# Transform pieces at other steps: where a schedule written out by hand puts the FFT pieces between the matmuls of the next layer

## The chip, the cores and the metric

One core of one Trainium2 chip. The metric is device time in microseconds of one execution; the median of three runs is compared.

## The reference

A Fourier filter along the sequence, and then a feed-forward layer with a leaky activation. Eight batches, 3008 positions, 256 channels, 2048 hidden units.

```python
batch, seq, dim = (8, 3008, 256)
X = np.fft.rfft(x, axis=1)
Y = X * (filt_r + 1j * filt_i)[None, :, :]
y = np.fft.irfft(Y, n=x.shape[1], axis=1)          # float32
h = y.reshape(24064, 256) @ moe_w_in               # 256 -> 2048
g = np.maximum(h, 0.0) + moe_alpha * np.minimum(h, 0.0)
out = (g @ moe_w_out).astype(np.float32)           # 2048 -> 256
```

## The kernel before, in words

The layer runs on 48 blocks of 512 (or 384) positions. A block takes 16 **steps**, 768 steps in all; 96 steps go over one batch. In a step the kernel issues first what its plan has for that step, then `up(j)` of the current block (two matmuls into `hps`, L478; after every second step ScalarE takes them out into `gtb`, L486, and VectorE applies the activation, L489 and L490), then the matmuls of the block before, a sixteenth of them. Some blocks (FAST, every second one from block 12, and the last ones) multiply by `wout` with seven products in place of eight (`seven`, L537); they need sums of quarters of `gtb`, `sums(w, h)`: z1 and z2 by VectorE (L498, L500) into `ss`, and two additions by DMA from GpSimd (L502, L504). The tuple SUMS says at which step of its block (counted from the block's first) each is issued.

Between them stand the **pieces** of the Fourier transform of the coming batches, split as 47 x 64. For each batch:

- `load_x` (L148): four x loads from GpSimd, with a cast, into four buffers `xs`. For batch b+1 they are put at steps p+6, p+10, p+16 and p+20, where p = 96(b-1) for batch b.
- `piece_a`, 16 times (L190): one matmul on `xs`; ScalarE takes the result into one of two buffers `asb`. After every fourth, `save_a` (L195) writes a buffer to DRAM (`a_dram`) from SyncE.
- `turn_a` (L202): four reads of `a_dram` with rows and columns exchanged, 384 KB each in runs of 512 bytes, into `at`. SyncE issues them once the last write has landed and the last reader of `at` is done. This is the turned array.
- `piece_b`, 12 times, the forward pairs kp = 0 to 11 (L210): two matmuls on `at`; VectorE multiplies the result by the filter into `ww` and `uu` (L213, L214); then two DMAs from GpSimd add the halves of `ww` onto `uu` (L216).
- `piece_c`, 12 times, the inverse pairs (L228): two matmuls on `uu`; ScalarE takes the result into `v`. After every third, `turn_c` (L237) writes to `v_dram` in four DMAs from SyncE; after the last of them three `load_z` (L246) read it back into `zt`, on the same queue. A fourth `load_z` follows later.
- `piece_d`, 16 times (L253): four matmuls on `zt`; ScalarE takes the result into `yT`, which `up` reads. The batch of this plan is read from step p+96 on.

Pieces a, b, c and d share two PSUM banks; the string BANKS says for each piece, in the order of issue, which one it uses. STEPS_A, STEPS_B, STEPS_C and STEPS_D give the steps of the four kinds of pieces relative to p, for batches with index 3 to 7 (index 3 has its own list of a, and its b not before 2 kp - 12). Index 0, 1 and 2 have plans of their own (`plan_fft`). The steps of a for batch b+1 fall into the steps of batch b: step -84 of it is p+12.

All engines issue in the order of the program. SyncE carries the output stores (L447), L195, L202, L237 and L246; GpSimd carries L148, L216, L502 and L504. A tile with several buffers is reused in turn: the write of a new one waits for the readers of the old one. `uu` has four buffers, `ww` three, `at` and `v` one, `zt` three.

Of the kernel before, what the change touches and what calls it, by code (L numbers as in the profile page):

```python
# [20 lines left out]
NH = 32  # L21
BANKS = (
    "010101010101010101010101010101001011100011011010100100100101010101010101010101010101010101010101"
    "010101010101010101010010101010101000111101010010010010101011010101011101010101010101010100011001"
    "011010110011010101011001101011010101010101010100101010110010110010101010101001100101001010101010"
    "101010110101010011010011010101010101100110101101010101010101010010101011001011001010101010100110"
    "01010010101010101010101010110010101001100100101010101010"
)
STEPS_A = (-81, -80, -78, -72, -70, -67, -62, -61, -56, -52, -52, -50, -50, -45, -44, -42)
STEPS_B = (-20, -16, -9, 3, 7, 16, 29, 36, 40, 47, 57, 57)  # L30
STEPS_C = (-1, 5, 12, 14, 21, 33, 37, 48, 63, 63, 66, 66)
STEPS_D = (83, 85, 85, 86, 89, 93, 94, 99, 105, 107, 109, 118, 119, 129, 139, 146)
FAST = frozenset([n for n in range(12,42) if n%6 in (0,2,4)]+[42,43,44,45])
SUMS = ((11, 1, 0), (12, 3, 0), (17, 1, 1), (18, 3, 1), (19, 2, 0), (19, 2, 1), (20, 4, 0), (20, 4, 1))
TAIL = ((12, 1, 0), (12, 3, 0), (18, 1, 1), (18, 3, 1), (18, 2, 0), (18, 2, 1), (20, 4, 0), (21, 4, 1))
LAG = 16
AF = mybir.ActivationFunctionType
# [43 lines left out]
def kernel(  # L81
# [63 lines left out]
    def load_x(b, c):  # L145
        xs = p_x.tile([2 * N1, 8 * D], FP16, name="xs")
        for h in range(2):
            nc.gpsimd.dma_start(out=xs[h * N1 : h * N1 + N1], in_=xrow(b, h, c))  # L148
        return xs
# [445 lines left out]
    def put(step, fn, *args):  # L595
        plan.setdefault(step, []).append((fn, args))

    def plan_fft(b, a0, ga, ta, b0, gap, add, lag, d0, quarters, x_at):
        f = Fft(b)
        for i in range(16):  # L600
            put(int(a0 + ga * i), f.piece_a, i, on_act)
        for c in range(4):
            put(int(a0 + ga * (4 * c + 3)), f.save_a, c)
            if b + 1 < NB:
                put(x_at[c],
                    lambda b=b, c=c: xc.update({(b + 1, c): load_x(b + 1, c)}))
        for q in range(quarters):
            w = NK1 // quarters
            put(ta, f.turn_a, nc.sync, w * q, w * q + w)
        bs = [b0 + (2 * int(gap * kp / 2) if add else int(gap * kp)) for kp in range(12)]  # L610
        for kp in range(12):
            put(bs[kp], f.piece_b, kp)
            put(bs[kp] + lag, f.piece_c, kp, on_act)
        for q in range(4):
            put(bs[3 * q + 2] + lag + 1, f.turn_c, q)
        for i in range(16):
            put(d0 + min(i, 4) + 2 * max(i - 4, 0), f.piece_d, i, on_act)
        put(d0 + 5, f.load_z, 3)
# [9 lines left out]
    for i in range(4):  # L628
        put(26 + 3 * i, neg, 6 * i, 6 * i + 6)
    plan_fft(1, 16, 1, 32, 40, 3, 0, 6, 92, 4, (20, 24, 74, 75))  # L630
    plan_fft(2, 66, 2, 97, 109, 4.5, 8, 12, 187, 4, (110, 114, 118, 122))
    for b in range(3, NB):
        p = 96 * (b - 1)
        f = Fft(b)
        steps_a = STEPS_A if b > 3 else [int(2.4 * i) - 68 if i < 8 else 2 * i - 60 for i in range(16)]
        steps_b = STEPS_B if b > 3 else [max(st, 2 * kp - 12) for kp, st in enumerate(STEPS_B)]
        for i in range(16):
            put(p + steps_a[i], f.piece_a, i, on_act)
            if i % 4 == 3:
                put(p + steps_a[i] + 1, f.save_a, i // 4)  # L640
        if b + 1 < NB:
            for c in range(4):
                put(p + (6, 10, 16, 20)[c], lambda b=b, c=c: xc.update({(b + 1, c): load_x(b + 1, c)}))
        put(p + steps_a[15] + 4, f.turn_a, nc.sync)
        for kp in range(12):
            put(p + steps_b[kp], f.piece_b, kp)
            put(p + STEPS_C[kp], f.piece_c, kp, on_act)
            if kp % 3 == 2:
                put(p + STEPS_C[kp] + 1, f.turn_c, kp // 3)
        for i in range(16):  # L650
            put(p + STEPS_D[i], f.piece_d, i, on_act)
        put(p + STEPS_D[3] + 2, f.load_z, 3)

# [19 lines left out]
    for n, (p, t0, tn, _) in enumerate(blocks):  # L673
        old, blk = blk, Block(n, p, t0, tn)
        if blk.fast:
            for at, w, h in SUMS if n < 39 else TAIL:
                ahead.setdefault(16 * n + at, []).append((blk, w, h))
# [51 lines left out]
```

## Time and profile before

| what | value |
|---|---|
| median of 3 runs | 815.16 us (814.38 to 817.88) |
| the profiled execution, its own time | 818.72 us |
| its span from the first to the last instruction | 816.9 us |
| mean granted TensorE clock | 0.983 |
| busy: TensorE, VectorE, ScalarE, GpSimd | 775.0, 682.1, 608.5, 267.7 us |
| DMA | 120.84 MB, 148 GB/s over the span |

Busy times are those of the profiled execution. The granted clock is 1.00 where TensorE runs at its full clock; a stretch with 0.91 or 0.83 has a part of it at half of the clock. The names after an arrow in the view of waits are what ended the wait.

### The profile page before, as it was taken

Reading aid. Unit: us, or ns where it says so; the run is one execution under the profiler, and the core shown is the slowest. Engines: PE = TensorE matmul, PEld = TensorE weight load, DVE = VectorE, ACT = ScalarE, POOL = GpSimd, SP = SyncE. Lnnn points to the kernel's source line nnn. Section 1 sums busy time; section 2 is a strip of 40 time slices with the busy share of each in tenths; the row PEclk is TensorE's granted clock in tenths of the full one; section 3 lists DMA queues with packets and bytes.
Section 4 is the critical chain, followed back from the end, with each engine's and each line's share of the span. In section 5 each row is a group of like instructions: output and inputs, shape, how many; then the busy total and the mean of one; then the engine's idle time right before and its main releaser. Section 6 shows DMA issues by size and latency. Waiting matters only on the chain. (4 is left out here: it accounts for less than half of the span.)

```text
span 816.9 us, 18100 instructions
## 1 busy us (share of the span) xinstructions
PE 775.0 (95%) x6856; PEld 545.7 (67%) x6856; DVE 682.1 (83%) x1489; ACT 608.5 (74%) x896; POOL 267.7 (33%) x353
## 2 busy tenths in 40 slices
PE   7999988999999997999899997999979999999998
PEld 6856655666676664766667664766657777677766
DVE  4788885789788895998989896898969999879994
ACT  4787677878778784888768885688857777677773
POOL 7720450153124350362333432343414235102210
PEclk9999999999999998999999998999999999999999
DMA  9995566685767878697886969669788456544642
GB/s 192 186 201 160 109 124 179 159 153 108 170 166 140 158 151 203 119 173 156 168 203 130 173 150 191 150 106 185 157 186 174 89 107 107 129 121 94 131 90 69
DMA packets 113807, 120.84 MB, mean 148 GB/s; under 512 B 12648, under 2 KB 94328, under 8 KB 113592
## 3 DMA queue, kind: packets, MB, share of 16 engines
q0 software_dynamic: 33584, 50.09, 37.8%
q1 hardware_dynamic: 79992, 69.52, 32.0%
q8 instruction: 54, 0.88, 0.4%
q14 instruction: 33, 0.27, 0.1%
q10 hardware_dynamic: 144, 0.07, 0.0%
HBM read 56.06 MB, written 46.66 MB: 126 GB/s over the span
## 5 line engine op out<-in xcount | busy, mean ns | idle before, releaser
L486 ACT ACTIVATE gtb<-hps 128x1024 f16<-128x1024 f32 (+1 forms) x384 | 385.7, 1005 | 108.7 <-PE hps L478 105.6
L478 PE MATMUL hps<-yT,win_s 128*128 128x512 f16 (+1 forms) x1536 | 454.2, 378 | 0.4 <-ACT gtb L486 0.2
L489 DVE TENSOR_SCALAR m<-gtb,alm_s 128x512 f16<-128x512 f16 (+1 forms) x768 | 235.5, 348 | 93.6 <-ACT gtb L486 91.4
L490 DVE TENSOR_TENSOR gtb<-gtb,m 128x1024 f16<-128x1024 f16 (+1 forms) x384 | 261.6, 681 | 16.9 <-PE op L537 0.5
L515 PE MATMUL op<-wout_s,gtb 128*128 128x256 f16 x1728 | 265.8, 275 | 0.0
L216 POOL DMA_DIRECT2D uu<-ww x168 | 141.9, 1018 | 332.9 <-DVE uu L214 142.2
L515 PEld LDWEIGHTS <-gtb 128*128 128x128 f16 x1728 | 170.4, 99 | 117.3 <-issue 5.1
L478 PEld LDWEIGHTS <-win_s 128*128 128x128 f16 x1536 | 137.8, 99 | 31.5 <-issue 7.1
L537 PEld LDWEIGHTS <-gtb 128*128 128x128 f16 x1520 | 104.2, 98 | 50.8 <-DMA gtb<-ss 2.6
L502 POOL DMA_DIRECT2D gtb<-gtb x38 | 40.1, 1056 | 153.1 <-DVE m L489 112.3
L537 PE MATMUL op<-wout_s,gtb 128*128 128x128 f16 x912 | 78.3, 220 | 2.3 <-DMA gtb<-ss 1.7
L260 ACT ACTIVATE asb<-psF 96x512 f16<-96x512 f32 x112 | 65.4, 592 | 12.8 <-PE psF L190 8.5
L260 ACT ACTIVATE v<-psF 128x512 f16<-128x512 f32 x84 | 49.5, 596 | 31.2 <-PE psF L228 31.1
L260 ACT ACTIVATE yT<-psF 128x376 f16<-128x376 f32 x120 | 57.2, 487 | 19.7 <-PE psF L253 19.2
L213 DVE TENSOR_TENSOR ww<-psF,filts_s 128x512 f16<-128x512 f32 x84 | 57.3, 682 | 0.0
L214 DVE TENSOR_TENSOR uu<-psF,filt_s 128x512 f16<-128x512 f32 x84 | 57.1, 680 | 0.0
L537 PEld LDWEIGHTS <-ss 128*128 128x128 f16 x608 | 42.7, 98 | 20.9
L148 POOL DMA_DIRECT2D xs<-in_x_dram x64 | 48.1, 994 | 20.0 <-PE psF L190 13.2
L537 PE MATMUL op<-tw_s,gtb 128*128 128x128 f16 x608 | 52.7, 219 | 0.0
L537 PE MATMUL op<-tw_s,ss 128*128 128x128 f16 x608 | 52.5, 219 | 0.0
L228 PE MATMUL psF<-uu,twi_s 128*128 128x256 f16 x168 | 31.8, 277 | 20.4 <-DMA uu<-ww 19.3
L190 PE MATMUL psF<-xs,wf_s 94*96 94x512 f16 x112 | 41.6, 383 | 5.4 <-ACT asb L260 3.6
(85 smaller groups left out, 518.1 us busy)
## 6 DMA issues: line engine op xcount, KB each, us to landing
out_dram<-osb SPq DMA_DIRECT2D x127, 128.0 KB
xs<-in_x_dram POOLq DMA_DIRECT2D x64, 188.0 KB, 6.9
a_dram<-asb SPq DMA_DIRECT2D x28, 384.0 KB
uu<-ww POOLq DMA_DIRECT2D x168, 64.0 KB, 2.9
v_dram<-v SPq DMA_DIRECT2D x112, 96.0 KB
zt<-v_dram SPq DMA_DIRECT2D x28, 384.0 KB
gtb<-gtb POOLq DMA_DIRECT2D x38, 256.0 KB, 4.1
gtb<-ss POOLq DMA_DIRECT2D x38, 256.0 KB, 6.0
```

Of the source, the lines that this page charges most:

```text
L148: nc.gpsimd.dma_start(out=xs[h * N1 : h * N1 + N1], in_=xrow(b, h, c))
L190: nc.tensor.matmul(ps[0:96], wf1_s, xs[:, o : o + 512], start=True, stop=True)
L213: nc.vector.tensor_mul(ww, px, filts_s[:, 2 * kp : 2 * kp + 2])
L214: nc.vector.tensor_mul(uu, px, filt_s[:, 2 * kp : 2 * kp + 2])
L216: nc.gpsimd.dma_start(out=uu[o : o + 64], in_=ww[64 - o : 128 - o], accum_op=OP.add)
L260: nc.scalar.activation(o, i, AF.Copy)
L478: nc.tensor.matmul(self.hps[:, j % 2, 0:tn], win_s[:, kt, j * 128 : (j + 1) * 128], yT[:, kt, self.t0 : self.t0 + tn], start=(kt == 0), st ...
L486: nc.scalar.activation(g, hs, AF.Copy)
L489: nc.vector.tensor_scalar(ms[:, i], g[:, i], 0.0, a, OP.min, OP.mult)
L490: nc.vector.tensor_add(g, g, ms)
L515: nc.tensor.matmul(op[:, si % 2], self.pair(k // 2)[:, k % 2, 128 * si : 128 * si + 128], wout_s[:, k], start=(k == 0), stop=(k == 15))
L537: nc.tensor.matmul(acc[:, 128 * i : 128 * i + 128], x[:, k, 128 * i : 128 * i + 128], b[:, k], start=first and k + i == 0, stop=k == 7, sk ...
```

## The change

The four lists of steps, the list of sums and the string of banks are replaced. Relative to p, with the step of the batch in which they run:

- Forward pairs (b), kp 0 to 11: from -20, -16, -9, 3, 7, 16, 29, 36, 40, 47, 57, 57 to -21, -15, 4, 6, 13, 21, 25, 27, 32, 40, 54, 55.
- Inverse pairs (c): from -1, 5, 12, 14, 21, 33, 37, 48, 63, 63, 66, 66 to 2, 10, 16, 19, 24, 33, 35, 46, 62, 63, 70, 70. The last two stand 16 and 15 steps behind their forward pairs (9 before).
- The read of the turned array, four steps behind the last a: from p+58 to p+57. The writes to `a_dram`, one step behind every fourth a, move with them: p+25, 36, 47, 55 become p+21, 39, 46, 54.
- The first a of the next batch: from p+15 to p+12. The x loads stay.
- The d pieces start at 89 in place of 83 and end at 147 in place of 146; the fourth `load_z` goes from 88 to 93.
- The a pieces of batch index 3 have one spacing (2.4 steps) all along; its last eight are closer to the others and end two steps earlier, and with them its read of the turned array.
- For batch index 2, piece a 7 and the second write to `a_dram` (c = 1) go from step 80 to step 79. Step 80 also holds the last `turn_c` of batch index 1 with its three `load_z`.
- SUMS: z1 of the first half at 9 (11), its addition at 10 (12), z2 of the first half at 16 (19), the second half's addition at 17 (18), the last DMA addition at 21 (20).

```diff
-STEPS_A = (-81, -80, -78, -72, -70, -67, -62, -61, -56, -52, -52, -50, -50, -45, -44, -42)
-STEPS_B = (-20, -16, -9, 3, 7, 16, 29, 36, 40, 47, 57, 57)
-STEPS_C = (-1, 5, 12, 14, 21, 33, 37, 48, 63, 63, 66, 66)
-STEPS_D = (83, 85, 85, 86, 89, 93, 94, 99, 105, 107, 109, 118, 119, 129, 139, 146)
+STEPS_A = (-84, -81, -77, -76, -65, -59, -58, -58, -56, -53, -52, -51, -50, -48, -46, -43)
+STEPS_B = (-21, -15, 4, 6, 13, 21, 25, 27, 32, 40, 54, 55)
+STEPS_C = (2, 10, 16, 19, 24, 33, 35, 46, 62, 63, 70, 70)
+STEPS_D = (89, 89, 90, 91, 92, 94, 95, 98, 100, 101, 105, 113, 118, 125, 144, 147)
...
-SUMS = ((11, 1, 0), (12, 3, 0), (17, 1, 1), (18, 3, 1), (19, 2, 0), (19, 2, 1), (20, 4, 0), (20, 4, 1))
+SUMS = ((9, 1, 0), (10, 3, 0), (16, 2, 0), (17, 1, 1), (17, 3, 1), (19, 2, 1), (20, 4, 0), (21, 4, 1))
...
-            put(int(a0 + ga * i), f.piece_a, i, on_act)
+            put(int(a0 + ga * i) - (b == 2 and i == 7), f.piece_a, i, on_act)
...
-            put(int(a0 + ga * (4 * c + 3)), f.save_a, c)
+            put(int(a0 + ga * (4 * c + 3)) - (b == 2 and c == 1), f.save_a, c)
...
-        steps_a = STEPS_A if b > 3 else [int(2.4 * i) - 68 if i < 8 else 2 * i - 60 for i in range(16)]
+        steps_a = STEPS_A if b > 3 else [int(2.4 * i) - 68 for i in range(16)]
```

The new lines of BANKS, one digit a piece in the new order of issue, are left out here.

More of the change, by code (lines that the diff above doesn't have):

```diff
@@ L23 @@
     "010101010101010101010101010101001011100011011010100100100101010101010101010101010101010101010101"
[L24 to L27, printed above, removed]
-)
-STEPS_A = (-81, -80, -78, -72, -70, -67, -62, -61, -56, -52, -52, -50, -50, -45, -44, -42)
-STEPS_B = (-20, -16, -9, 3, 7, 16, 29, 36, 40, 47, 57, 57)
-STEPS_C = (-1, 5, 12, 14, 21, 33, 37, 48, 63, 63, 66, 66)
-STEPS_D = (83, 85, 85, 86, 89, 93, 94, 99, 105, 107, 109, 118, 119, 129, 139, 146)
+    "010101010101010101010010101010101000111101010011001011101010010101010101010110001101001010010101"
+    "010110101001010101010101101001010100100100101010010101010110101001010100101010100101101010110110"
+    "110101011010101010010101101010110101010110100101010010010010101001010101011010100101010010101010"
+    "01011010101101101101010101010010101010100110101010101010"
+)
+STEPS_A = (-84, -81, -77, -76, -65, -59, -58, -58, -56, -53, -52, -51, -50, -48, -46, -43)
+STEPS_B = (-21, -15, 4, 6, 13, 21, 25, 27, 32, 40, 54, 55)
+STEPS_C = (2, 10, 16, 19, 24, 33, 35, 46, 62, 63, 70, 70)
+STEPS_D = (89, 89, 90, 91, 92, 94, 95, 98, 100, 101, 105, 113, 118, 125, 144, 147)
 FAST = frozenset([n for n in range(12,42) if n%6 in (0,2,4)]+[42,43,44,45])
-SUMS = ((11, 1, 0), (12, 3, 0), (17, 1, 1), (18, 3, 1), (19, 2, 0), (19, 2, 1), (20, 4, 0), (20, 4, 1))
+SUMS = ((9, 1, 0), (10, 3, 0), (16, 2, 0), (17, 1, 1), (17, 3, 1), (19, 2, 1), (20, 4, 0), (21, 4, 1))
 TAIL = ((12, 1, 0), (12, 3, 0), (18, 1, 1), (18, 3, 1), (18, 2, 0), (18, 2, 1), (20, 4, 0), (21, 4, 1))
```

## The prediction

> **What bounds the kernel now.** I read the page's header and busy line first, then the waits of the TensorE, then busy time in stretches of 20 us, and last the timeline around the stretches that fall short.
>
> ```profile
> span 816.9 us, 18100 instructions
> ...
> PE 775.0 (95%) x6856; PEld 545.7 (67%) x6856; DVE 682.1 (83%) x1489; ACT 608.5 (74%) x896; POOL 267.7 (33%) x353
> ```
>
> TensorE (PE) is busy 95% of the span; the next engine, VectorE (DVE), 83%. In most stretches PE is the bound, so what it loses in waits is lost to the end. Which waits, from the view of waits (total us, times, longest):
>
> ```profile
> PE psF L228 <- DMA uu<-ww: 19.3, 9, 5.1
> PE psF L190 <- ACT asb L260: 3.6, 2, 3.2
> PE psF L253 <- DMA zt<-v_dram: 2.0, 1, 2.0
> PE op L537 <- DMA gtb<-ss: 1.7, 4, 1.1
> PE psF L190 <- DMA xs<-in_x_dram: 0.5, 1, 0.5
> ACT asb L260 <- DMA a_dram<-asb: 3.8, 1, 3.8
> DVE m L489 <- ACT gtb L486: 91.4, 119, 6.7
> ```
>
> The large one is L228, an inverse pair (piece_c) that waits for the DMA adding ww onto uu. The stretches show where (columns: stretch; its length; PE, PEld, DVE, ACT, POOL busy; granted PE clock; DMA share; GB/s):
>
> ```profile
> 120.00:140.00 20.00, 16.15 (x120) 11.56 (x120) 9.92 (x27) 13.71 (x23) 3.23 (x6) 1.00 0.76 198
> 140.00:160.00 20.00, 20.00 (x161) 13.55 (x160) 13.17 (x32) 16.76 (x28) 0.52 (x1) 0.91 0.49 140
> ...
> 300.00:320.00 20.00, 15.58 (x119) 9.88 (x118) 12.12 (x27) 10.30 (x14) 3.40 (x4) 0.83 0.84 188
> ...
> 340.00:360.00 20.00, 20.00 (x169) 13.67 (x167) 18.70 (x43) 17.02 (x27) 7.63 (x11) 1.00 0.65 114
> ...
> 400.00:420.00 20.00, 17.39 (x140) 12.01 (x139) 15.59 (x36) 12.88 (x17) 3.84 (x5) 1.00 0.86 192
> ...
> 500.00:520.00 20.00, 14.88 (x89) 9.10 (x86) 10.31 (x24) 8.23 (x10) 0.00 (x0) 0.83 0.83 197
> ...
> 600.00:620.00 20.00, 15.63 (x102) 10.12 (x100) 12.52 (x29) 9.75 (x11) 1.24 (x2) 0.91 0.90 207
> ...
> 700.00:720.00 20.00, 18.03 (x165) 13.54 (x164) 14.76 (x35) 12.38 (x20) 3.52 (x4) 0.91 0.75 175
> ```
>
> Once a batch, near 300, 400, 500 and 600 us, PE stands still, and afterwards the clock is granted below 1.00. The loss of a stretch is its idle time plus 20 x (1 - clock): 4.4 + 3.4 = 7.8, then 2.6, then 5.1 + 3.4 = 8.5, then 4.4 + 1.8 = 6.2, together 25.1 us. A stretch between them (340 to 360) loses nothing, though DVE is at 18.70 of 20 in it. One such place in the timeline:
>
> ```profile
> 492.72 0.60 PE L210 MATMUL psF<-at,twf_s 128*128 128x256 f16 x4
> ...
> 495.60 3.40 POOL L216 DMA_DIRECT2D uu<-ww  x4 [4.26 <-DVE uu L214]
> ...
> 496.43 2.54 SPq L202 DMA_DIRECT2D at<-a_dram  x4
> ...
> 506.55 0.61 PE L228 MATMUL psF<-uu,twi_s 128*128 128x256 f16 x2 [5.12 <-DMA uu<-ww]
> ```
>
> Both last forward pairs of the batch (L210, kp 10 and 11, step p+57) run at 492.72; their four uu DMAs leave POOL from 495.60 to 499.0; SP issues the read of the turned array (L202) at 496.43, into the middle of them. The inverse pair of kp 11 stands nine steps behind and gets its data at 506.55, 13.8 us after L210.
>
> **The change, part by part.** No instruction is added or removed; only order moves. Steps below are relative to p = 96(b-1).
>
> *Inverse pairs 10 and 11 (p+66 to p+70) and their forward pairs (p+57 to p+54 and p+55).* The distance grows from 9 to 16 and 15 steps. A step costs 0.91 to 1.00 us (worked out below), so the inverse pair of kp 11 comes 13.7 to 15 us after its forward pair. Even if the DMA is as late as the worst above, 13.8 us, the wait is 0.1 us. It should be earlier: the read moves by one step only (p+58 to p+57), the forward pairs by two and three, so the POOL DMAs leave mostly ahead of it. Four waits go: **-25.1 us**. What is late next there: the turn into v_dram and the zt loads follow at p+71 (from p+67), but their readers L253 move too, from p+83 to p+89.
>
> *First read of x in the next batch (L190).* Its first piece moves from step -81 to -84, in the running batch from p+15 to p+12, while its load stays at p+6. This is the side of the change that costs.
>
> ```profile
> 438.49 0.38 PE L210 MATMUL psF<-at,twf_s 128*128 128x256 f16 x2
> ...
> 442.82 1.68 POOL L148 DMA_DIRECT2D xs<-in_x_dram  x2
> ...
> 450.51 0.38 PE L190 MATMUL psF<-xs,wf_s 94*96 94x512 f16 x1
> ```
>
> ```profile
> 538.87 0.38 PE L210 MATMUL psF<-at,twf_s 128*128 128x256 f16 x2
> ...
> 544.88 1.76 POOL L148 DMA_DIRECT2D xs<-in_x_dram  x2
> ...
> 550.32 0.39 PE L190 MATMUL psF<-xs,wf_s 94*96 94x512 f16 x1 [0.51 <-DMA xs<-in_x_dram]
> ```
>
> ```profile
> 545.41 4.78 DMA xs<-in_x_dram
> ```
>
> The L210 rows are kp 3 at p+3, the L190 rows the first piece at p+15, twelve steps later: 12.0 us in one batch, 10.9 (without the 0.5 wait) in the other, whence 1.00 and 0.91 us a step. POOL is in order: the x load stands behind the uu DMAs of the forward pair just ahead of it, in the new kernel kp 2 at p+4. The second half lands 4.78 us after its issue (the third fence, from the chain of waits; its issue, 545.41, is 0.53 behind the first). Counted from L210 that is 442.82 + 0.53 + 4.78 - 438.49 = 9.6 us, or 550.19 - 538.87 = 11.3 us. The new distance from p+4 to p+12 is eight steps, 8.0 or 7.3 us. So PE waits 1.6 to 4.0 us, in each of four batches (loads for b = 4 to 7). I take the smaller landing, because in the other POOL stood longer for its queue: 2 x 1.6 + 2 x 2.3 = 7.8, less the 0.5 that is there already, **+7.3 us**; ends: +2 if DVE, with no forward pair at -9 any more, is a microsecond earlier, and 2 x 3.3 + 2 x 4.0 = 14.6.
>
> *Clock after those waits.* In the stretches a wait of 1.97 us (700:720) was followed by 0.91, that is 1.8 us, and one of 2.61 (400:420) by 1.00. I take one dip in four waits: **+1.8 us**, ends 0 and 7.2. [...]
>
> *Last batch, inverse output pieces (L253, p+83 to p+89).*
>
> ```profile
> 702.86 2.04 SPq L237 DMA_DIRECT2D v_dram<-v  x4
> ...
> 708.39 1.28 SPq L246 DMA_DIRECT2D zt<-v_dram  x3
> ...
> 712.57 0.34 PE L253 MATMUL psF<-wi_s,zt 96*128 96x94 f16 x4 [1.97 <-DMA zt<-v_dram]
> ```
>
> L253 moves by six steps, 5.5 us. The v_dram writes are put four steps later, 3.6 us, but at 702.86 SP had only come to them from output stores whose data was late, so they move less. The 1.97 us and the 1.8 us of clock in 700:720 go: **-3.8 us**, ends -3.8 and 0.
>
> *One array write of batch index 2 (put one step earlier with its piece).*
>
> ```profile
> 125.06 2.75 SPq L237 DMA_DIRECT2D v_dram<-v  x4
> ...
> 130.88 1.25 SPq L246 DMA_DIRECT2D zt<-v_dram  x3
> ...
> 132.22 0.38 SPq L195 DMA_DIRECT2D a_dram<-asb  x1
> ...
> 138.41 0.59 ACT L260 ACTIVATE asb<-psF 96x512 f16<-96x512 f32 x1 [3.85 <-DMA a_dram<-asb]
> ```
>
> The write (L195) stood at step 80, on SP behind the four v_dram writes and the three zt loads of the same step, which wait for those writes to land. At step 79 it goes ahead of them, some 6.5 us earlier, and its buffer is free when ScalarE (ACT) wants it. PE's 3.2 us wait and the 1.8 us of clock in 140:160 go, 5.0. What is late next: L253 at step 92 needs the zt loads, which move back by the write's SP time, 0.4 to 1 us, and with the stall gone arrives 3 us earlier against a load issued at 130.88 that needs 4.2 us (708.39 to 712.57 above). I give 1.5 back: **-3.5 us**, ends 0 and -5.0.
>
> *The sums of the seven-product blocks (SUMS).* z1 and z2 come up to three steps earlier, a12's second addition one step later in program order and in blocks 18, 24, 30 behind the x load at p+20. Its cover is the ten steps until L537 uses it. The waits now are 1.7 us in all; I take 0, ends -1.7 and +5 (three blocks by the 1.76 us that POOL needs for two halves of an x load).
>
> *Denser forward pairs (p+13, 21, 25, 27, 32 instead of p+7, 16, 29, 36, 40) and other banks.*
>
> ```profile
> L213 DVE TENSOR_TENSOR ww<-psF,filts_s 128x512 f16<-128x512 f32 x84 | 57.3, 682 | 0.0
> ...
> L214 DVE TENSOR_TENSOR uu<-psF,filt_s 128x512 f16<-128x512 f32 x84 | 57.1, 680 | 0.0
> ```
>
> Each pair gives DVE 1.36 us and holds one of two PSUM banks until DVE is done. Four of them now fall into eleven steps: 5.4 us in some 10.5 us. DVE waits for ACT 119 times (91.4 us), so it catches up often, but here it will run 2 to 3 us behind, and a bank that is wanted again after three steps can wait: **+1.5 us** (0.3 in each of five batches), ends 0 and +6.
>
> **Sum.** -25.1 + 7.3 + 1.8 - 3.5 - 3.8 + 1.5 = -21.8 us. The profiled execution took 818.72 us (span 816.9), so 796.9; from the median of the runs, 815.16, it is 793.4. The profiled one is 3.6 us above that median, and I can't tell how much of this lies in the waits that go, so I take the middle: **795 us**.
>
> **Rivals.**
>
> *All waits go and the x load is in time.* For it: the first L190 of one batch had to spare 450.51 - 448.1 = 2.4 us (448.1 = 442.82 + 0.53 + 4.78), against three steps that it loses, 2.7 to 3.0. Then -25.1 - 5.0 - 3.8 + 2 = -32, 783 to 787.
>
> *The x load costs its upper end.* 14.1 us net and four dips, 7.2: -25.1 + 21.3 - 3.5 - 3.8 + 1.5 = -9.6, 805 to 809. For it: the longer landing was in a batch that had the shorter steps.
>
> *The stalls stay in other dress.* The read of the turned array slows whatever is in flight: L537's addition issued at p+52 and p+53 instead of uu. With 4 us a batch lost there and at the zt loads, five batches, plus a dip each, 29: nothing is left, 812 to 818. Against it: the addition is put four and five steps ahead of the read.
>
> *Slower.* The inverse pair of kp 6 follows its forward pair by ten steps, 9.1 to 10 us, and that one now stands behind kp 5, the second addition and an x load on DVE, POOL and the DMA queue. From a landing of 10 us on it makes PE wait. If kp 4, 5 and 6 wait 2.5 us each with one dip, 9.3 us in five batches, 46: about 839. Against it: in the trace only DMAs that met the turned array took so long, and DVE has idle time on both sides.
>
> *No effect* can't be: the order of every engine changes.
>
> **How the numbers follow.** Forecast 0.60 (788 to 802), clean 0.13, upper x load 0.15, other dress 0.06, slower 0.06. Half a per cent, about what a measurement can tell from no change here, is 4 us: faster holds the first three and a little of the fourth, 0.89; same 0.05; slower 0.06. The range leaves out the last two and the edge of the clean one: 785 to 808.
>
> **What would show it.** Right: no row of some us for L228 waiting for uu near 300, 400, 500, 600 us; a new row, PE L190 waiting for xs, four times, 6 to 10 us in all; no wait for a_dram by ACT near 135; no zt wait near 710; clock at 1.00 in those stretches. Wrong: L228 still waits over 5 us, at kp 10 and 11 or at kp 4 to 6; or L190 waits over 14 us; or PE's idle time is gone and the span isn't, which would mean that DVE was the bound beneath.

## The result, and the profile after

| | before | after |
|---|---|---|
| median of 7 runs each | 815.17 us (812.13 to 820.57) | 808.08 us (803.52 to 811.70) |
| ratio | | 0.9896, 95% interval 0.9855 to 0.9937 |
| profiled execution: its time, span | 818.72, 816.9 us | 803.52, 801.7 us |
| its mean granted clock | 0.983 | 1.000 |

The change makes the kernel faster by 1.0% (0.6 to 1.5), some 8 us, where 20 were forecast; 808.08 lies at the upper edge of the range, just outside. The profiled pair shows 15.2 us, because the one of after is the fastest of its seven runs, 4.6 us below their median, and the one of before lies 3.6 us above its own. What the timed runs lack beside it is mostly clock: their spans go from 801.7 and 803.9 us at a mean clock of 1.000 over 804.6 at 0.998 and 806.3 at 0.994 to 809.9 at 0.991. In the profile of before the clock stands at half in six stretches after the start, four of 3.41 us (a dip) and two of 6.83 (counted as two dips); by that length and the half clock one dip costs 1.7 us and takes 0.002 off the mean.

The waits of TensorE (PE) after (total us, times, longest):

```profile
PE psF L190 <- DMA xs<-in_x_dram: 8.7, 4, 2.7
PE op L537 <- DMA gtb<-ss: 5.6, 4, 2.0
PE psF L253 <- ACT yT L260: 3.5, 4, 1.9
PE psF L228 <- DMA uu<-ww: 2.9, 5, 1.1
...
PE psF L190 <- ACT v L260: 2.5, 4, 0.8
```

L228's wait for uu fell from 19.3 to 2.9 us. All of that lies between 80 and 115 us, in the batch with index 1, whose steps the change leaves alone. The waits for `a_dram` and for zt are gone. But the others shown here are new or have grown: for xs (0.5 us before), for the addition into gtb (1.7), for yT (0.7) and for v (1.1). The stretches that stalled before, and the ones that stall now (stretch; length; PE, PEld, DVE, ACT, POOL busy; clock; DMA; GB/s):

```profile
120.00:140.00 20.00, 19.87 (x158) 14.40 (x159) 11.81 (x31) 17.40 (x31) 2.86 (x5) 1.00 0.75 194
240.00:260.00 20.00, 16.54 (x142) 11.19 (x140) 15.79 (x34) 14.34 (x23) 9.30 (x13) 1.00 0.69 116
300.00:320.00 20.00, 20.00 (x166) 14.15 (x165) 18.25 (x42) 14.79 (x20) 4.10 (x5) 1.00 0.93 201
340.00:360.00 20.00, 17.62 (x162) 11.88 (x159) 18.01 (x39) 15.63 (x25) 13.81 (x19) 1.00 0.96 171
360.00:380.00 20.00, 18.00 (x148) 12.15 (x145) 17.00 (x37) 14.90 (x23) 6.06 (x9) 1.00 0.67 138
400.00:420.00 20.00, 20.00 (x167) 13.99 (x165) 18.37 (x41) 13.82 (x17) 5.34 (x7) 1.00 0.96 224
...
520.00:540.00 20.00, 16.09 (x142) 10.75 (x140) 15.64 (x36) 13.25 (x22) 6.47 (x9) 1.00 0.56 105
550.00:570.00 20.00, 18.20 (x160) 12.55 (x158) 17.17 (x37) 15.24 (x24) 6.26 (x8) 1.00 0.76 146
600.00:620.00 20.00, 20.00 (x207) 14.31 (x205) 18.70 (x42) 15.88 (x25) 7.00 (x8) 1.00 0.85 196
```

PE is busy throughout at 300, 400 and 600 us, where it lost 2.6 to 7.8 us. In exchange 240 to 260 loses 3.5, 340 to 360 2.4, 360 to 380 2.0, 520 to 540 3.9 and 550 to 570 1.8, where the same stretches lost at most 0.5 before. That these waits cost no clock (1.00 in every stretch above) is the luck of this execution: five of the six other timed runs have a lower mean clock, down to 0.991. What the luck consists of was not shown. The timeline of one x load:

```profile
431.83 0.38 PE L210 MATMUL psF<-at,twf_s 128*128 128x256 f16 x2
...
435.32 1.67 POOL L216 DMA_DIRECT2D uu<-ww  x2 [13.65 <-DVE uu L214]
436.38 1.69 POOL L148 DMA_DIRECT2D xs<-in_x_dram  x2
...
441.83 0.39 PE L190 MATMUL psF<-xs,wf_s 94*96 94x512 f16 x1 [1.89 <-DMA xs<-in_x_dram]
```

As foreseen, the load leaves POOL 4.6 us after the forward pair kp 2 (L210), behind its uu DMAs, and L190 starts 10.0 us after L210, 1.9 of them waited. And the turned array:

```profile
486.66 0.38 PE L210 MATMUL psF<-at,twf_s 128*128 128x256 f16 x2
489.43 3.41 POOL L216 DMA_DIRECT2D uu<-ww  x4 [3.12 <-DVE uu L214]
490.31 3.56 SPq L202 DMA_DIRECT2D at<-a_dram  x4
...
499.88 0.60 PE L228 MATMUL psF<-uu,twi_s 128*128 128x256 f16 x4
```

Still the read (L202) starts in the middle of the four uu DMAs; only the distance has grown. The inverse pairs come at 499.88, 13.2 us behind the last forward pair, and wait for nothing.

### The profile page after: what moved, and what is told of

Same layout as the page of the kernel before. It is cut to its first block, busy times and chain, and to the rows that moved or that the text cites. A ratio compares the mean times of both kernels' runs of the same rounds, so it can differ in the third digit from the quotient of the medians.

```text
span 801.7 us, 18106 instructions
## 1 busy us (share of the span) xinstructions
PE 763.5 (95%) x6856; PEld 539.4 (67%) x6856; DVE 683.2 (85%) x1489; ACT 605.2 (75%) x896; POOL 267.4 (33%) x353
## 4 chain that ended last, share of the span: by engine, by line
PE 68%; DMA 12%; DVE 8%; ACT 4%; POOL 3%; issue 3%; SPq 0%; DVEq 0%; ACTq 0%; POOLq 0%
PE hps L478 30%; PE op L515 18%; PE op L537 9%; DMA gtb<-ss 5%; PE psF L190 3%; ACT gtb L486 3%; DVE m L489 2%; DMA xs<-in_x_dram 2%; PE psF L253 2%; PE psF L228 2%; DVE gtb L490 2%; DMA out_dram<-osb 2%; PE psF L210 1%; POOL uu L216 1%; POOL xs L148 1%
## 5 line engine op out<-in xcount | busy, mean ns | idle before, releaser
L478 PE MATMUL hps<-yT,win_s 128*128 128x512 f16 (+1 forms) x1536 | 449.2, 374 | 0.4 <-ACT gtb L486 0.2
L515 PE MATMUL op<-wout_s,gtb 128*128 128x256 f16 x1728 | 262.0, 272 | 0.0
L537 PEld LDWEIGHTS <-gtb 128*128 128x128 f16 x1520 | 103.5, 98 | 53.6 <-DMA gtb<-ss 6.3
L502 POOL DMA_DIRECT2D gtb<-gtb x38 | 37.9, 998 | 176.1 <-DVE ss L498 70.0
L537 PE MATMUL op<-wout_s,gtb 128*128 128x128 f16 x912 | 77.5, 219 | 6.1 <-DMA gtb<-ss 5.6
L260 ACT ACTIVATE asb<-psF 96x512 f16<-96x512 f32 x112 | 66.0, 593 | 21.3 <-PE psF L190 21.3
L537 PEld LDWEIGHTS <-ss 128*128 128x128 f16 x608 | 42.6, 98 | 20.9
L190 PE MATMUL psF<-xs,wf_s 94*96 94x512 f16 x112 | 42.0, 381 | 12.6 <-DMA xs<-in_x_dram 8.7
L537 PE MATMUL op<-tw_s,gtb 128*128 128x128 f16 x608 | 52.5, 219 | 0.0
L537 PE MATMUL op<-tw_s,ss 128*128 128x128 f16 x608 | 52.5, 219 | 0.0
L253 PE MATMUL psF<-wi_s,zt 96*128 96x94 f16 x504 | 41.1, 204 | 3.8 <-ACT yT L260 3.5
```

Of the source, the lines that this page charges most:

```text
L190: nc.tensor.matmul(ps[0:96], wf1_s, xs[:, o : o + 512], start=True, stop=True)
L253: nc.tensor.matmul(ps[:, m], self.zt[g][:, 4 * mh + m, dh * 128 : dh * 128 + 128], wi3_s, start=True, stop=True)
L260: nc.scalar.activation(o, i, AF.Copy)
L478: nc.tensor.matmul(self.hps[:, j % 2, 0:tn], win_s[:, kt, j * 128 : (j + 1) * 128], yT[:, kt, self.t0 : self.t0 + tn], start=(kt == 0), st ...
L515: nc.tensor.matmul(op[:, si % 2], self.pair(k // 2)[:, k % 2, 128 * si : 128 * si + 128], wout_s[:, k], start=(k == 0), stop=(k == 15))
L537: nc.tensor.matmul(acc[:, 128 * i : 128 * i + 128], x[:, k, 128 * i : 128 * i + 128], b[:, k], start=first and k + i == 0, stop=k == 7, sk ...
```

## The experiments

**The changed kernel once more.**

> The changed kernel once more, for a second profile and more times. Theory A (new waits, and clock dips behind them in most executions): a median of 806 to 810 again, and a profile that is not the luckiest execution shows L190 waiting for xs for 8 to 10 us, L537 for the addition for 4 to 7, and one to four stretches of 3.4 us at half clock. Theory B (nothing waits much more than in the profile; the executions differ by something else, such as VectorE as the next bound): the same waits, clock 1.00, yet a longer span.

808.15 us (805.78 to 812.83, 6 runs), ratio 0.9912 (0.9884 to 0.9940). The second profile (span 804.9):

```profile
PE psF L190 <- DMA xs<-in_x_dram: 10.5, 4, 3.4
PE psF L253 <- ACT yT L260: 3.8, 4, 1.8
PE op L537 <- DMA gtb<-ss: 3.6, 3, 1.7
PE psF L228 <- DMA uu<-ww: 3.3, 5, 1.2
```

The same waits, the x load's a little above what theory A expects and the addition's a little below. The runs: 805.78 and 806.67 us at clock 0.998, 807.08 at 0.996, 809.23 at 0.994, 810.97 at 0.993, 812.83 at 0.989. Theory A holds: the waits repeat, and the runs differ by clock.

**The first x load earlier.**

```diff
-                put(p + (6, 10, 16, 20)[c], lambda b=b, c=c: xc.update({(b + 1, c): load_x(b + 1, c)}))
+                put(p + (0, 10, 16, 20)[c], lambda b=b, c=c: xc.update({(b + 1, c): load_x(b + 1, c)}))
```

> The changed kernel with the first x load of a batch at p+0 in place of p+6, ahead of the uu DMAs of kp 2. A: the wait of L190 for xs (8.7 us in the profile) goes, and with it most clock dips: 797 to 801. B: the time is lost elsewhere, 805 to 809, because VectorE or another DMA is late next.

796.41 us (794.54 to 798.45, 4 runs), ratio 0.9761 (0.9737 to 0.9785), against the same runs of before as the run above: the difference of the two ratios is 0.0151 of 815.6, **12.3 us** (9 to 15, from both intervals). That is theory A, and slightly more than it expects. L190 no longer waits for xs; the largest that are left:

```profile
PE op L537 <- DMA gtb<-ss: 5.0, 4, 2.3
PE psF L253 <- ACT yT L260: 3.8, 4, 1.9
PE psF L228 <- DMA uu<-ww: 3.0, 4, 1.2
```

The waits themselves were 8.7 and 10.5 us in the two profiles; the middle clock is 0.998 here against 0.995 in the run above, and that difference is 2.4 us.

**The old list of sums in the changed kernel.**

```diff
-SUMS = ((9, 1, 0), (10, 3, 0), (16, 2, 0), (17, 1, 1), (17, 3, 1), (19, 2, 1), (20, 4, 0), (21, 4, 1))
+SUMS = ((11, 1, 0), (12, 3, 0), (17, 1, 1), (18, 3, 1), (19, 2, 0), (19, 2, 1), (20, 4, 0), (20, 4, 1))
```

> The changed kernel with the old list of sums, so that the last DMA addition of a seven-product block stands ahead of the x load at p+20 again. A: L537's wait for the addition falls from 5.6 to about 2 us, 3 to 4 us faster than the changed kernel, 803 to 806. Rival (the earlier z1 and z2 are worth more than the place behind the x load): 808 to 812.

811.38 us (806.98 to 821.73, 10 runs), ratio 0.9952 (0.9921 to 0.9983): 3.3 us slower than the changed kernel by the ratios, but the intervals overlap. The profiled execution is the slowest of the ten (821.73), so only the times are read. Theory A fails here as it was put: the old list does put the addition ahead of the x load, yet it is not faster. So the rest of the new list makes up for about what the addition loses, or for more. Which of its steps does that (z1 and z2 come earlier in it) wasn't tried.

**The inverse pairs alone.** The kernel before, with one edit:

```diff
-STEPS_C = (-1, 5, 12, 14, 21, 33, 37, 48, 63, 63, 66, 66)
+STEPS_C = (-1, 5, 12, 14, 21, 33, 37, 48, 63, 63, 70, 70)
```

> The kernel before with one edit: inverse pairs 10 and 11 at p+70 in place of p+66. All else as before, the x load's wait too. A: the four stalls at L228 go alone, 20 to 25 us: 790 to 796, faster than the whole change. B: a good part of the stalls' time is only moved: 803 or more.

798.72 us (796.39 to 800.16, 4 runs), ratio 0.9786 (0.9761 to 0.9811): **17.4 us** (15.4 to 19.5), twice what the whole change brings. It lies between what A and B expect, nearer to A. Its stretches:

```profile
300.00:320.00 20.00, 18.59 (x156) 12.77 (x154) 16.77 (x38) 14.02 (x19) 4.04 (x5) 1.00 0.80 178
400.00:420.00 20.00, 19.60 (x169) 13.64 (x168) 17.72 (x39) 14.13 (x20) 5.74 (x8) 1.00 0.92 215
500.00:520.00 20.00, 18.76 (x205) 14.41 (x203) 18.63 (x43) 14.10 (x24) 8.55 (x10) 1.00 0.89 206
600.00:620.00 20.00, 20.00 (x217) 14.51 (x216) 19.39 (x43) 16.79 (x27) 6.93 (x10) 1.00 0.73 163
```

Of the 25.1 us that these four stretches lost, 3.1 stay, as waits without a dip. So 22 went in the profiled pair, whose times differ by 22.3 us; in the timed runs 17.4 came. The profiled pair is a lucky one: 818.72 is 3.2 us above the median of the runs of before, and 796.39 is the fastest of these four, 2.3 us below theirs. Nothing else is changed, so the four stalls are what the change lives on, and the rest of it, taken together, costs more than it brings.

**The fourth x load behind the addition**, with the first one early:

```diff
-                put(p + (6, 10, 16, 20)[c], lambda b=b, c=c: xc.update({(b + 1, c): load_x(b + 1, c)}))
+                put(p + (0, 10, 16, 22)[c], lambda b=b, c=c: xc.update({(b + 1, c): load_x(b + 1, c)}))
```

> The changed kernel with the x loads of a batch at p+0, 10, 16, 22 in place of p+6, 10, 16, 20: the first is early as in the run before this (796.4 us), the fourth now stands behind the last DMA addition of the seven-product block. A: L537's waits for the addition (5.0 us there) fall below 2, another 3 to 4 us and a clock dip: 791 to 794. Rival (VectorE or the rest of the queue is late next): 796, no change from that run.

793.12 us (790.59 to 796.55, 6 runs), ratio 0.9712 (0.9684 to 0.9740): by the ratios 4.0 us faster than with the first load alone, as theory A expects, though the intervals just touch. What the edit undoes is seen on POOL in the changed kernel, where the two additions (L504) of one block stand around the two halves of the x load:

```profile
450.29 1.23 POOL L504 DMA_DIRECT2D gtb<-ss  x1
450.84 1.75 POOL L148 DMA_DIRECT2D xs<-in_x_dram  x2
452.02 1.49 POOL L504 DMA_DIRECT2D gtb<-ss  x1
```

and who waits for the second:

```profile
462.81 0.23 PE L537 MATMUL op<-wout_s,gtb 128*128 128x128 f16 x1 [0.77 <-DMA gtb<-ss]
```

It left POOL at 452.0 and was awaited at 462.8, 10.8 us later, against 6.0 us from issue to landing in the median of all such DMAs (4.0 to 11.9). With the x load behind it:

```profile
443.94 1.23 POOL L504 DMA_DIRECT2D gtb<-ss  x1
445.50 0.85 POOL L504 DMA_DIRECT2D gtb<-ss  x1 [0.32 <-PE psF L210]
...
450.08 1.66 POOL L148 DMA_DIRECT2D xs<-in_x_dram  x2
```

and L537's waits are 1.8 us in all. So the addition gets its place ahead of the x load back, and this time, with the rest of the new list kept, some 4 us come with it.

**The output pieces spread.**

```diff
-STEPS_D = (89, 89, 90, 91, 92, 94, 95, 98, 100, 101, 105, 113, 118, 125, 144, 147)
+STEPS_D = (87, 88, 90, 91, 93, 94, 95, 98, 100, 101, 105, 113, 118, 125, 144, 147)
```

(with the first x load at p+0)

> The first x load at p+0, and the first output pieces (L253) at 87, 88, 90, 91, 93 in place of 89, 89, 90, 91, 92, in the same order and banks. Burst theory: the wait of L253 for ScalarE's yT (3.8 us) comes from two pieces in one step and goes: 793 to 795. Queue theory: ScalarE there waits for an output store that stands on SyncE behind the zt loads; the wait stays, under this or another line, 796.

798.36 us (794.76 to 800.13, 6 runs), ratio 0.9765 (0.9736 to 0.9794): no change from 0.9761. L253's wait for yT went from 3.8 to 2.0 us, but L537's rose from 5.0 to 6.5. A wait of 0.8 us for zt also came, but at 136 us, in batch index 2, whose output pieces the edit leaves alone. The times are those of the queue theory. The chain that it names is read off one timeline. In the changed kernel's last batch:

```profile
694.27 1.26 SPq L246 DMA_DIRECT2D zt<-v_dram  x3
695.98 3.88 SPq L447 DMA_DIRECT2D out_dram<-osb  x5
...
703.33 0.38 ACT L551 ACTIVATE osb<-op 128x256 f32<-128x256 f32 x1 [1.98 <-DMA out_dram<-osb]
703.61 0.86 ACT L260 ACTIVATE yT<-psF 128x376 f16<-128x376 f32 x2
704.51 0.33 PE L253 MATMUL psF<-wi_s,zt 96*128 96x94 f16 x4 [1.86 <-ACT yT L260]
```

SyncE holds the output stores until the zt loads are issued (694.27 to 695.53, the stores from 695.98); ScalarE waits 1.98 us for a store to free its osb; the two yT behind it come late, from 703.61; L253 waits 1.86 us for their bank. This wait of 1.86 us stands where the one of 1.97 us for zt stood before. That another order on SyncE would end it is not shown; none was tried.

**Two edits to the kernel before**: the inverse pairs at p+70, and the array write of batch index 2 with its piece one step earlier.

```diff
-            put(int(a0 + ga * i), f.piece_a, i, on_act)
+            put(int(a0 + ga * i) - (b == 2 and i == 7), f.piece_a, i, on_act)
...
-            put(int(a0 + ga * (4 * c + 3)), f.save_a, c)
+            put(int(a0 + ga * (4 * c + 3)) - (b == 2 and c == 1), f.save_a, c)
```

> The kernel before with inverse pairs 10 and 11 at p+70 (798.7 us alone) and, beside it, piece a 7 and the second array write of batch index 2 at step 79. A: the wait for that write goes with its clock dip, 4 to 5 us: 794 to 795. Rival (the zt loads behind it are late next and take it back): 798.

793.69 us (791.82 to 796.85, 6 runs), ratio 0.9715 (0.9691 to 0.9739), 5.8 us below the first edit alone by the ratios. The clock was 1.000 in four of six runs. These two edits do nearly three times what the whole change does.

**Both repairs of the x loads and the spread together.**

> The changed kernel with the x loads at p+0, 10, 16, 22 and the output pieces spread as in the other run. If the three costs add: 787 to 791. If VectorE (683 us busy) or the queues are next: 794 to 796.

794.79 us (793.43 to 795.15, 4 runs), ratio 0.9722 (0.9696 to 0.9747): no better than the repairs of the x loads alone, where 787 to 791 stood for costs that add. They don't.

**The kernel before once more.**

> The kernel before once more, for a second profile. If the profile that was priced is typical: L228 waits some 19 us for uu and five or six stretches at half clock follow, 25 us in the four stretches. If it was an unlucky one: fewer of either, nearer to 18 us, which is what taking these stalls out alone brought in the timed runs (about 17).

817.15 us (811.82 to 820.20, 8 runs), ratio 1.0005 (0.9967 to 1.0043). Its profile (span 815.5):

```profile
300.00:320.00 20.00, 15.46 (x120) 10.02 (x118) 12.46 (x28) 10.61 (x15) 3.40 (x4) 0.83 0.80 180
400.00:420.00 20.00, 17.60 (x130) 11.56 (x127) 14.12 (x34) 11.75 (x17) 2.92 (x5) 0.91 0.83 191
500.00:520.00 20.00, 15.87 (x109) 10.35 (x107) 12.44 (x29) 10.36 (x14) 1.20 (x2) 0.91 0.88 203
600.00:620.00 20.00, 16.17 (x108) 10.60 (x107) 13.08 (x30) 10.05 (x13) 2.54 (x3) 0.91 0.88 202
```

By the same reading 7.9 + 4.2 + 5.9 + 5.6 = 23.7 us against 25.1, and L228 waited 17.5 us for uu against 19.3. So the stalls of the first profile come back nearly whole. But both profiles of before have a mean clock of 0.983; of the 17 runs of before that stand beside them, from 810.82 us at 0.996 to 821.30 at 0.983, the middle one has 0.987. So by their mean clock the profiles are of executions with about two dips, 3.4 us, more than the middle one of those 17 (one dip more than the middle one of the eight here, 0.985).

**A third edit to the two.**

```diff
-STEPS_D = (83, 85, 85, 86, 89, 93, 94, 99, 105, 107, 109, 118, 119, 129, 139, 146)
+STEPS_D = (85, 86, 87, 87, 89, 93, 94, 99, 105, 107, 109, 118, 119, 129, 139, 146)
```

> The kernel before with inverse pairs 10 and 11 at p+70, the array write of batch index 2 at step 79, and the first four output pieces at 85, 86, 87, 87 in place of 83, 85, 85, 86. The last waits of any size in the run without the third edit are L253 for the zt loads (4.5 us in three batches). If they go and nothing takes their place: 789 to 791. If something else is late next: 793 to 794, no change.

795.35 us (793.50 to 797.51, 6 runs), ratio 0.9761 (0.9724 to 0.9799), no better than without it. The zt waits went from 4.5 us to 0.4, and these came:

```profile
PE psF L228 <- DMA uu<-ww: 5.1, 7, 1.3
PE op L537 <- DMA gtb<-ss: 4.4, 6, 1.2
PE psF L253 <- ACT yT L260: 3.6, 6, 0.7
```

## Why the prediction was wrong

The sign was right, and so were most of the mechanisms: the four stalls go, the new wait of L190 for xs comes, the waits for `a_dram` and zt go. What failed is the size of five terms and one chain that was missed. The sum came to -21.8; the timed runs give -7 to -8.5. The largest failure is the first one: the four stalls were priced at 25.1 us off one execution and were worth 17.4.

- **The stalls at the inverse pairs, -25.1.** They go, but alone they are worth 17.4 us (15.4 to 19.5) in the timed runs. Some 3 us stay as shorter waits when the pairs stand 13 steps apart; that leaves 22. The rest of the difference lies in which executions were profiled: 3.2 us between the profile of before and the median of its runs, 2.3 between the profile with the one edit and its median. Most of these 5.5 us is clock, 0.983 against 0.987 and 0.998 against 0.997, together 4.1 us. The prediction saw a difference of 3.6 us between the profile and the median; taking the middle let half of it stand. The first reason given, that the POOL DMAs would leave mostly ahead of the read, is wrong (489.43 to 492.84 against 490.31); the second, that the distance alone is enough, held.
- **The x load, +7.3 and +1.8 for the clock.** The waits were 8.7 and 10.5 us, inside the reading of rows (9.6 us from L210 to landing; 10.0 measured). The whole, with the clock, is 12.3 us (9 to 15) by the run that removes it: the term was some 3 us too small, near the edge of what the runs can tell.
- **The sums, 0.** Here the working was at fault: the place behind the x load was seen, and priced by POOL's issue time alone, as an upper end of 5. In the queue the addition took 10.8 us in place of 6, and PE waited 5.6 and 3.6 us in the two profiles, against 1.7 (4.6 of the 5.6 in the three blocks that the prediction names); the run with the x load behind it gives 4 us back.
- **Denser pairs and banks, +1.5.** L190 waits 2.5 us for ScalarE's v where it waited 1.1, L253 3.5 to 3.8 for yT where it waited 0.7: 4.2 to 4.5 in all. The waits end with ScalarE, not with VectorE as the term has it; the largest one, 1.9 us, is where output stores stand on SyncE behind the zt loads. That chain was missed: the working of -3.8 for the last batch moved the loads and L253, and didn't ask what stands behind the loads on their queue.
- **The array write, -3.5.** In the profile step 96 comes 5.7 us earlier, 0.6 of it from before the first step, and the edit brings 5.8 in the times when it is put on top of the first one. The 1.5 us given back for the zt loads weren't lost in the profile of after; in three other kernels with this edit L253 waits 0.8 to 1.7 us for them there.

Put in place: -17.4 - 5.8 - 1.9 (zt, net of the wait that stands there now) + 12.3 + 4 + 2.3 (the other waits for ScalarE) = -6.5, close to what was measured. This is bookkeeping and not a proof: the terms come from different kernels, and two of the runs show that such terms don't simply add.

On the clock, the prediction took one dip in four waits, from two waits of one execution, 2.60 and 1.97 us. These are the stretches at half clock of that profile, the longest wait within or shortly before each, and three long waits with none behind them:

| execution | wait of TensorE, its end | clock at half |
|---|---|---|
| before | 1.46 us, 20.67 | 20.98 to 24.40 |
| before | 3.15 us, 139.05 | 140.45 to 143.86 |
| before | 3.51 us, 312.94 | 311.12 to 317.94 |
| before | 2.60 us, 408.00 | none |
| before | 5.12 us, 506.55 | 505.68 to 512.50 |
| before | 4.37 us, 605.25 | 604.66 to 608.08 |
| before | 1.97 us, 712.57 | 713.89 to 717.30 |
| after | 2.10 us, 345.11 | none |
| after | 2.72 us, 537.82 | none |

Length alone doesn't part them: 1.97 us was followed by a dip, 2.60 and 2.72 were not. In the second profile of before, 400 to 420 with 2.4 us of idle time and 700 to 720 with 1.9 have a clock of 0.91 each; in the second one of after the waits for xs reach 3.4 us, and its mean clock, 0.998, leaves room for about one dip. The six starts in before lie 35, 50, 57, 29 and 32 times 3.413 us apart. What decides whether a wait costs clock was not shown.

Of the rivals the upper x load (805 to 809) came closest in time, by luck: it priced the x load at 21.3 us, which was 12.3, and left the stalls at 25.1, which were 17.4. The stalls in other dress gave a part: TensorE's idle time after the first step was 31.6 and 29.2 us in the two profiles of before and is 27.0 and 28.2 in those of after, 18.2 with the two edits alone. (Its price doesn't add up: 29 on top of the sum's -21.8 is 7 us slower than before, not 812 to 818.) Most of what the whole change brings is the clock: usually 0.987 before and 0.996 after, 7 us of 815.

## What to carry to other kernels

When a stall is taken out by moving work, try the one move that takes it out by itself first: here two small edits give 2.8% and the whole rearrangement, which contains moves to the same ends, 1.0%. Where a DMA moves behind another on one queue (here the second addition behind an x load, 10.8 us in place of 6.0), price it by the landing of what is now ahead of it, and follow what waits behind it on that queue, output stores too. A loss read off one profile is worth that much only if the profiled execution is the usual one: compare its time and clock with those of all the runs before pricing, and do the same for the profile that it is set against.

## What the runs showed of the hardware that was not expected

The spread of single executions, 810.8 to 821.3 us before, goes with the mean clock: 0.996 in the fastest, 0.983 in the slowest. One kernel loses clock in one execution and none in another: the changed kernel has a span of 801.7 us at 1.000, with 27 us of idle time in pieces of up to 2.7 us, and one of 809.9 us at 0.991 in another execution. Why was not shown: a wait of 1.97 us was followed by a stretch of 3.41 us at half clock, and one of 2.72 was not. The two edits, whose longest wait after the first step is 1.7 us, stay at 1.000 or 0.998 in all six runs.

All of the best versions, by different ways, end at 793 to 796 us, with 17 to 19 us of idle time in their profiles, and further edits move the waits about. What holds them there wasn't found.
